# Two levels of Strassen instead of one in the first channel product, with outer sums added on the way out of PSUM

## The chip, the cores and the metric

The kernel runs on one core of a Trainium2 chip. Five engines work beside each other, each through its own list of instructions in order: TensorE (PE; its weight loads are shown apart as PEld), VectorE (DVE), ScalarE (ACT), GpSimd (POOL) and SyncE (SP), whose list issues nearly all DMAs. SBUF holds tiles of 128 partitions; matmuls write PSUM, which has eight banks of 512 float32 columns. The metric is the device time of one execution in microseconds. Three runs of the kernel before took 1167.77, 1168.61 and 1169.41 us; the median is 1168.61.

## The reference

Two blocks follow each other, all in float32.

```python
# attention: q, k, v are (8, 8, 576, 64), omega is (128, 64)
q_p, k_p = (phi(q_s), phi(k_s))       # exp(h - max h) / sqrt(m), h = x @ omega.T - |x|^2 / 2
kv = np.einsum('bhsm,bhsd->bhmd', k_p, v)
num = np.einsum('bhsm,bhmd->bhsd', q_p, kv)
den = np.einsum('bhsm,bhm->bhs', q_p, z)[..., None] + 1e-06
# bridge: (8, 8, 576, 64) -> x of (8, 576, 512); then a Fourier mix and a channel MLP
X = np.fft.fft(np.fft.fft(x, axis=1), axis=2)
u = x + np.real(X)
un = (u - mu) / np.sqrt(var + 1e-06)
ch = np.maximum(un @ w_ch1, 0.0) @ w_ch2      # w_ch1 (512, 2048), w_ch2 (2048, 512)
return u + ch
```

The change concerns the first of the two products of the last lines, `un @ w_ch1` with its relu: 4608 tokens, 512 channels in, 2048 hidden channels out.

## The kernel before

The kernel has two stages. In the first (to 424 us of the profile) it does the attention, the Fourier mix and four plain tiles of 128 tokens of the MLP. It also prepares for the second stage: the weights w1 stay in SBUF, and the sums that the second channel product needs of w2 are written to DRAM as 49 tiles of 256 KB (`w2l`).

In the second stage the other 4096 tokens go through the MLP in eight blocks (j = 0 to 7) of 512 tokens. A product of matrices is computed by Strassen's scheme in Winograd's form: the two operands are cut into 2 x 2 parts, sums of the parts are formed (`sums_left`, `sums_right`), seven products of half size are taken instead of eight, and the four parts of the result are sums of these. The products are numbered 1 to 7 in the code; 1, 2, 4 and 7 have a left factor that is a part or a simple difference, 5, 6 and 3 have sums.

The first channel product of a block uses one level. The left factor is w1 (channels by hidden, transposed by the matmul), the right one the normalized tokens `unT`. `first_of(j, fc)` does one of eight slices of 2 x 128 hidden channels: seven products of two matmuls each, 128 hidden channels by 256 tokens. Three results are saved from PSUM by ACT (`save`, L1324), three are evicted by DVE, which adds the saved one and applies the relu in one custom operation (`added`, L1296), and one goes out by ACT (L1362). They land in `hid`. POOL then forms the four sums of hidden parts that the second product needs (L1377). The weight sums (`weight_sums`, L1254) are made once and stay in SBUF as `w1s`.

The second channel product of a block uses two levels, 7 x 7 products ("leaves") of four matmuls, 128 tokens by 128 channels each. `product_of(j, i)` does the seven leaves of one outer product i; DVE forms the inner sums of hidden tokens (`add_up`, L1457), ACT and DVE empty PSUM (L1465, L1470, L1523), and POOL or DVE add the outer product's result into the residual rows (`plus`, L1530). The 49 weight tiles are read from DRAM again for each block (`loads_w2`, L1393) into twelve buffers (`wl`), so that SP's list reads ahead by up to twelve leaves.

While a block is computed, the next one is normalized: rows are read back from DRAM, DVE takes mean and variance (L1022 to L1024), POOL the power -1/2 (L1026), DVE scales (L1028) and transposes 32 x 32 blocks (L972), and the rows go through DRAM once more to arrive as `unT` (L980, L988).

The order of instructions on each engine is planned when the kernel is built. Work is written as streams of `Step`s, each with an engine, an estimated time, events that it waits for and buffers that it takes and gives. `Listing.run` takes the step that can begin first by these estimates, with small biases. In the first stage a string of picks (`PICKS`) fixes the choice. The estimates include a resource `PORT`: a step marked `port=True` on DVE or POOL is planned to start only when the last such step of either engine has ended. Three outer products or slices may be under way together (`set`).

## Time and profile before

| what | value |
|---|---|
| median of three runs | 1168.61 us |
| the profiled execution: span, the only time that the page gives of it | 1172.2 us |
| PE busy | 1153.5 us (98%) |
| DVE, ACT, POOL busy | 754.7, 436.8, 430.4 us |
| DMA | 220.34 MB, mean 188 GB/s |
| first stage, 0 to 424 us: PE, DVE, POOL busy | 413.4, 339.7, 173.9 us |
| block 3 (701.0 to 794.6 us): PE, DVE, ACT, POOL busy | 92.6, 52.6, 19.4, 32.5 us |

A line of the page names the program's line, the engine, the operation and the tiles (written <- read). Busy times of different engines overlap each other. In the chain of waits each piece ended last at its time, so that its lines add up to the span. "Idle before" is time that an engine spent waiting just before an instruction of a group, with the engine or DMA that ended the wait.

### The profile page before, as it was taken

To read this page: it belongs to the slowest core of one execution; us is meant where nothing else is said; L and a number is where in the kernel's file an instruction comes from. 1 tells how busy PE (TensorE), PEld (TensorE's weight loads), DVE (VectorE), ACT (ScalarE), POOL (GpSimd) and SP (SyncE) were. 2 spreads that over 40 slices of the span, in tenths; PEclk is the share of its full clock that TensorE was granted. 3 is DMA by queue.
4 is the path that set the end of the run, shared out by engine and by line. 5 is a ranking of instruction groups with operands and counts; after the bars stand their busy time and mean duration, and the time that the engine had idled before them with its cause. 6 is when DMAs were issued, how large, how long until landed. Compare 5 with 4: busy or idle time off the path is not lost.

```text
span 1172.2 us, 31328 instructions
## 1 busy us (share of the span) xinstructions
PE 1153.5 (98%) x12437; PEld 1032.9 (88%) x12437; DVE 754.7 (64%) x1573; ACT 436.8 (37%) x1485; POOL 430.4 (37%) x496
## 2 busy tenths in 40 slices
PE   8999999999999999999999999999999999999998
PEld 7888888779777868998998998898999899899898
DVE  5999999986676655744754664573573574474255
ACT  6998898866444212122112212212212212221211
POOL 2433444455472106225225324413513512522421
PEclk8999999999999999999999999999999999999999
DMA  7866765665662254873783593694495396388055
GB/s 218 224 188 186 240 181 178 203 210 163 207 196 101 77 162 139 263 264 85 222 278 112 172 308 99 152 317 141 112 319 190 82 290 231 83 258 263 35 166 203
DMA packets 167217, 220.34 MB, mean 188 GB/s; under 512 B 50080, under 2 KB 81056, under 8 KB 167072
## 3 DMA queue, kind: packets, MB, share of 16 engines
q1 hardware_dynamic: 166576, 218.09, 60.7%
q8 instruction: 98, 1.61, 0.6%
q14 instruction: 47, 0.39, 0.1%
q10 hardware_dynamic: 496, 0.26, 0.1%
HBM read 179.24 MB, written 43.25 MB: 190 GB/s over the span
## 4 chain that ended last, share of the span: by engine, by line
PE 88%; DMA 5%; DVE 4%; ACT 2%; SPq 1%; issue 1%; DVEq 0%
PE banks L1310 33%; PE banks L1490 27%; PE banks L1099 5%; PE banks L606 5%; PE banks L1122 4%; PE banks L512 4%; DMA wl<-w2l 3%; PE banks L640 2%; PE banks L687 2%; PE banks L849 2%; PE banks L799 1%; ACT e L566 1%; DVE nmx L549 1%; DMA kq<-in_k_dram 1%; PE banks L809 1%; PE banks L860 1%
## 5 line engine op out<-in xcount | busy, mean ns | idle before, releaser
L1490 PE MATMUL banks<-wl,sums 128*128 128x128 f32 x1792 | 217.4, 275 | 0.0
L1490 PEld LDWEIGHTS banks<-wl,sums 128*128 128x128 f32 x1792 | 208.6, 192 | 0.0
L1296 DVE CUSTOM_DVE_ANT_0 hid<-banks,s 128x256 f32<-128x256 f32 x192 | 80.9, 424 | 188.8 <-PE banks L1310 188.8
L566 ACT ACTIVATE e<-banks,nmx 128x128 f32<-128x128 f32 x576 | 165.3, 434 | 23.2 <-DVE nmx L549 22.4
L1324 ACT ACTIVATE s<-banks 128x256 f32<-128x256 f32 x192 | 73.7, 384 | 259.0 <-PE banks L1310 259.0
L1310 PE MATMUL banks<-unT,w 128*128 128x256 f32 x704 | 166.3, 379 | 0.0
L1310 PEld LDWEIGHTS banks<-unT,w 128*128 128x128 f32 x704 | 133.2, 190 | 18.3 <-issue 0.5
L1530 POOL TENSOR_TENSOR ur<-ur,part 128x512 f32<-128x512 f32 x32 | 47.3, 1479 | 267.1 <-ACT part L1523 187.0
L1465 ACT ACTIVATE s<-banks 128x128 f32<-128x128 f32 x168 | 46.6, 278 | 256.7 <-PE banks L1490 220.3
L1310 PE MATMUL banks<-tt,w1s 128*128 128x256 f32 x512 | 126.3, 379 | 0.0
L1310 PEld LDWEIGHTS banks<-tt,w1s 128*128 128x128 f32 x512 | 97.0, 190 | 13.7 <-DVE hid L1296 0.4
L1490 PE MATMUL banks<-wl,hid 128*128 128x128 f32 x768 | 100.0, 276 | 3.2 <-DMA wl<-w2l 3.1
L1470 DVE TENSOR_TENSOR part<-banks,s 128x128 f32<-128x128 f32 x168 | 49.0, 292 | 83.4 <-PE banks L1490 82.2
L549 DVE TENSOR_REDUCE nmx<-banks 128x8 f32<-128x1024 f32 (+1 forms) x96 | 89.3, 951 | 19.7 <-PE banks L606 15.5
L1490 PEld LDWEIGHTS banks<-wl,hid 128*128 128x128 f32 x768 | 94.0, 192 | 6.0 <-DMA wl<-w2l 4.5
L606 PE MATMUL banks<-om,kqT 64*64 64x128 f32 (+1 forms) x2088 | 80.6, 278 | 1.9 <-ACT kv L656 1.2
L1310 PE MATMUL banks<-unT,w1s 128*128 128x256 f32 x320 | 79.5, 379 | 0.0
L606 PEld LDWEIGHTS banks<-om,kqT 64*64 64x64 f32 (+1 forms) x2088 | 65.8, 140 | 13.3 <-issue 4.3
L1490 PE MATMUL banks<-wl,hs 128*128 128x128 f32 x576 | 75.1, 275 | 0.5 <-DVE part L1470 0.4
L1490 PEld LDWEIGHTS banks<-wl,hs 128*128 128x128 f32 x576 | 70.1, 192 | 1.2 <-DVE part L1470 0.6
L1377 POOL TENSOR_TENSOR hs<-hid,hs 128x256 f32<-128x256 f32 x64 | 50.1, 784 | 57.2 <-issue 37.1
L1310 PEld LDWEIGHTS banks<-unT,w1s 128*128 128x128 f32 x320 | 60.4, 190 | 8.7
(128 smaller groups left out, 1914.6 us busy)
## 6 DMA issues: line engine op xcount, KB each, us to landing
wl<-w2l SPq DMA_DIRECT2D x392, 256.0 KB
raw<-in_moe_w_ch_dram SPq DMA_DIRECT2D x32, 512.0 KB
kq<-in_k_dram SPq DMA_DIRECT2D x32, 288.0 KB
kq<-in_q_dram SPq DMA_DIRECT2D x32, 288.0 KB
vd<-in_v_dram SPq DMA_DIRECT2D x32, 288.0 KB
u<-us SPq DMA_DIRECT2D x36, 256.0 KB
ur<-us SPq DMA_DIRECT2D x36, 256.0 KB
out_dram<-ur SPq DMA_DIRECT2D x34, 256.0 KB
```

The source lines that it names most:

```text
L512: nc.tensor.transpose(ps[:, (j - j0) * 128 : (j - j0 + 1) * 128], src(j), ident[:])
L549: nc.vector.tensor_reduce(nmx[:, :, 0:num], pps[:, :, 0 : MF * num].rearrange("p b (c m) -> p b c m", m=MF), axis=AX.X, op=ALU.max, negate ...
L566: nc.scalar.activation(out=e[:, c + (i if num == 1 else 0), :], in_=pps[:, i, MF * c : MF * c + MF], func=AF.Exp, bias=nmx[:, i, c : c + 1],)
L606: nc.tensor.matmul(pps[cols, c, MF * m : MF * m + MF], lhsT=kqT[rows, j, cols], rhs=om2[rows, :],)
L1099: nc.tensor.matmul(hp[:, 0:TP], lhsT=w1[:, dc, 128 * fc : 128 * fc + 128], rhs=unTs[key][:, dc, :], start=(dc == 0), stop=(dc == NDC - 1),)
L1296: nc.vector._custom_dve(TENSOR_ADD_SAT, out=o, in0=ps, in1=sb, s0=FMAX, s1=0.0)
L1310: nc.tensor.matmul(ps[:, 0:HT].rearrange("f (b q) -> f b q", q=Q), lhsT=left(dc), rhs=right(dc), start=start and dc == 0, stop=(dc == D2 - 1),
L1324: nc.scalar.activation(out=s[:], in_=ps[:, 0:HT], func=AF.Copy)
L1377: nc.gpsimd.tensor_tensor(out=o, in0=l, in1=r, op=op)
L1470: nc.vector.tensor_tensor(out=part[:, t, 128 * m : 128 * m + 128], in0=ps[:, 0:128], in1=saved[with_][:], op=ALU.add,)
L1490: nc.tensor.matmul(ps[:, 0:128], lhsT=left[:, f], rhs=wls[j, i, n][:, f], start=start and f == 0, stop=(f == 3), skip_group_check=True,)
L1530: eng.tensor_tensor(out=o, in0=o, in1=other, op=ALU.add)
```

## The change

The first channel product now uses two levels in six of its seven outer products (in block 0: in one of the seven; the others, product 5 in every block and products 2 to 7 in block 0, stay undivided at the second level and are listed by `single`). `first_of(j, i)` does one outer product i over all 1024 hidden channels and 256 tokens of its part. A divided one has seven leaves of four matmuls, each 128 hidden channels by 128 tokens over 128 channels; the undivided one has sixteen matmuls of 256 tokens.

Outer products are no longer kept apart until all are there. Where one adds to an earlier result (`merged`: 6, 2, 7, 3, 4), DVE adds that result while it empties PSUM, and the last of each part (`final`: 2, 3, 4) gets the relu there too. Two sums are left for POOL (`u4_row`, `last_row`, the latter with a relu on ACT). `hid` is now four cells in the layout of the outer parts, and the four sums for the second product are formed in place in it by POOL (`left_sums`), each after the second product that still reads the cell.

DVE forms the inner sums of tokens for each block (`token_sums`). The weight sums of the outer products stay in SBUF (`so`, and one difference in place in w1); those of the inner level are formed in block 0 (`w1_sums`), stored to DRAM as 15 tiles of 256 KB (`w1l`), and read for each of blocks 1 to 7 into the same twelve buffers as the w2 tiles (`load_leaves`).

Besides: the second products are taken in another order, ACT instead of DVE scales the rows of the next block, saves of the second product have five buffers of their own (`sq`), the planner no longer regards `PORT` in the second stage, and streams have ranks that decide between steps that could start at the same time.

```diff
-SECOND = Clock(190.0, 0.15, 0.0, 0.1, {}, {}, (PE, ACT, DVE, POOL, SP, NONE), {})
+SECOND = Clock(190.0, 0.15, 0.0, 0.1, {}, {}, (PE, ACT, DVE, POOL, SP, NONE), {}, False)
...
-            return max(t, u, self.free[e] if e != NONE else 0.0, self.free[PORT] if step.on_port(e) else 0.0)
+            return max(t, u, self.free[e] if e != NONE else 0.0, self.free[PORT] if clock.port and step.on_port(e) else 0.0)
...
         nc.vector.bn_aggr(out=mv[:], in_=st[:])
         nc.vector.tensor_scalar(rstd[:], mv[:, 1:2], 1e-6, None, op0=ALU.add)
...
+        if block:
+            nc.vector.tensor_scalar(mv[:, 0:1], mv[:, 0:1], -1.0, None, op0=ALU.mult)
...
+        if block:
+            nc.gpsimd.tensor_tensor(mv[:, 0:1], mv[:, 0:1], rstd[:], op=ALU.mult)
+            yield Step(ACT, 0.6)
+            nc.scalar.activation(out=u[:], in_=u[:], func=AF.Identity, bias=mv[:, 0:1], scale=rstd[:])
+            yield from by_blocks(j, i, pool, u, *block)
+            return
         yield Step(DVE, 0.455, port=True)
         nc.vector.tensor_scalar(u[:], u[:], mv[:, 0:1], rstd[:], op0=ALU.subtract, op1=ALU.mult)
-        if block:
-            yield from by_blocks(j, i, pool, u, *block)
...
+    NB, TBIAS = 0.0, 0.6
+    ORDER1 = (1, 6, 5, 2, 7, 3, 4)
+    ORDER0 = (1, 2, 6, 5, 7, 3, 4)
+    def single(j):
+        return (5,) if j else ORDER0[1:]
+    def twice(j):
+        return tuple(i for i in ORDER1[1:] if i not in single(j))
...
+    def inner_tokens(j, i):
+        b11, b21, b22, b12 = (tokens(j, i, n) for n in (1, 2, 3, 7))
+        for o, l, r, op in sums_right(b11, b12, b21, b22, *(tokens(j, i, n) for n in (5, 6, 4))):
+            yield lambda o=o, l=l, r=r, op=op: nc.vector.tensor_tensor(out=o, in0=l, in1=r, op=op)
+    def token_sums(j):
+        if j == 1:
+            yield Step(NONE, after=tuple(("w1l", i, n) for i in twice(1) for n in (5, 6, 3)))
+        for i in (ORDER1 if j else ORDER0)[1:]:
+            if i in single(j):
+                continue
+            for m, op in enumerate(inner_tokens(j, i)):
+                yield Step(DVE, 0.28, after=(("tt", j),), makes=("tokens", j, i) if m == 3 else None, port=True, bias=TBIAS if j else -2.0)
+                op()
...
         for i, (o, l, r, op) in enumerate(ops):
-            yield Step(DVE, 0.6, makes=("tt", j) if i == 3 else None, port=True, bias=-0.49)
+            last = i == 3
+            yield Step(DVE, 2.0 if last else 0.7, makes=("tt", j) if last else None, port=True, bias=-0.49)
             nc.vector.tensor_tensor(out=o, in0=l, in1=r, op=op)
+            if last:
+                for inner in inner_tokens(j, 1):
+                    inner()
+        if pool is not mlpp:
+            yield from token_sums(j)
...
     listing.buffers = {k: [0.0] * n for k, n in dict(
-        slab=0, u=2, turn=1, ht=NFC, ur=3, s=6, set=3, wl=NWL, sums=NSUM, part=4,
+        slab=0, u=2, turn=1, ur=3, s=6, sq=5, set=3, wl=NWL, sums=NSUM, part=4,
     ).items()}
-    w1s += [late.tile([128, 3, D2, GW], F32, name=f"w1s{g}") for g in range(1, 4)]
-    hid = late.tile([128, NFC, TB], F32, name="hid")
-    hs = late.tile([128, HF, 3, HT], F32, name="hs")
+    hid = late.tile([128, 4, 2, 2, 4 * P], F32, name="hid")
+    so.update({i: late.tile([128, D2, F2], F32, name=f"so{i}") for i in (5, 6, 3)})
+    rx = late.tile([128, 6, 3, 4, Q], F32, name="rx")
...
+    READ = {1: 5, 6: 3, 5: 6, "u4": 7}
+    WITH = {6: C11, 2: C11, 7: C21, 3: C12, 4: C21}
+    BEFORE = {6: 1, 2: 1, 7: 6, 3: "u4", 4: 7}
...
+    def first_of(j, i):
+        me = ("first", j, i)
+        slot, read = slot_of(j, i), READ.get(i)
+        free = ((("second", j - 1, read), "read"),) if read and j else ()
+        merged, final = i in WITH, i in (2, 3, 4)
+        addend = slot_of(j, 1) if i in (6, 2) else WITH.get(i)
+        kept = {}
...
+            left, right = weights_of(j, i, n), tokens(j, i, n)
+            for f in range(4):
                 nc.tensor.matmul(
...
+                    ps[:, P * f : P * f + P].rearrange("f (b q) -> f b q", q=Q),
+                    lhsT=left[:, P * f : P * f + P],
+                    rhs=right,
+                    start=start and f == 0,
+                    stop=True,
                     skip_group_check=True,
                 )
...
+        def save(name, ps, f, t):
+            if merged:
+                yield Step(DVE, 0.7, 0.1, take=("s",), after=with_(f, t), makes=(me, name))
+            else:
+                yield Step(ACT, 0.6, 0.1, take=("s",), makes=(me, name))
+            s = late.tile([128, 4 * P], F32, name="s", tag="s", bufs=6)
+            if merged:
+                nc.vector.tensor_tensor(out=s[:], in0=ps, in1=cell_of(addend, f, t), op=ALU.add)
+            else:
+                nc.scalar.activation(out=s[:], in_=ps, func=AF.Copy)
+            kept[name] = s
+        def added(name, f, t, ps, saved, give, after=()):
+            yield Step(
+                DVE, 0.7, 0.1, after=((me, saved),) + free + over(f, t) + after, makes=(me, name), give=give + ("s",)
+            )
+            o = cell_of(slot, f, t)
+            if final:
+                relu_sum(o, ps, kept[saved][:])
+            else:
+                nc.vector.tensor_tensor(out=o, in0=ps, in1=kept[saved][:], op=ALU.add)
+            yield Fork(rest(f, t, (me, name)))
...
+        def u4_row(f, here):
+            read = ((("second", j - 1, READ["u4"]), "read"),) if j else tuple(
+                ("h", j, n, f, t) for n in (2, 6) for t in range(2)
+            )
+            yield from add(
+                row_of(C12, f), row_of(C21, f), row_of(slot, f), ALU.add,
+                after=here + read + tuple(("h", j, 6, f, t) for t in range(2)),
+            )
...
+                        cell = ps.rearrange("p (t n) -> p t n", t=2)[:, :, 128 * n : 128 * n + 128]
+                        for d in range(2):
+                            col = GW * f + 256 * c + 128 * n
+                            nc.tensor.matmul(
+                                cell.rearrange("f t (b q) -> f t b q", q=Q),
+                                lhsT=w[:, d, col : col + 128],
+                                rhs=right[:, :, d].rearrange("f (t b) q -> f t b q", t=2),
+                                start=n == 0 and d == 0,
+                                stop=d == 1,
+                                skip_group_check=True,
...
+        xb, x = yield from leaf(1, None, True, take=bank)
+        yield Fork(save("p1", x, 0, 0))
...
+    def left_sums(j):
+        for n, o, l, r, op, after in (
+            (3, C12, C11, C12, ALU.subtract, lambda f, t: (("h", j, 2, f, t), ("h", j, 3, f, t))),
+            (2, C22, C22, C12, ALU.subtract, lambda f, t: ((("second", j, 4), "read"), ("S", j, 3, f, t))),
+            (1, C11, C22, C11, ALU.add, lambda f, t: ((("second", j, 1), "read"), ("S", j, 2, f, t))),
+            (4, C21, C21, C22, ALU.subtract, lambda f, t: ((("second", j, 2), "read"), ("S", j, 2, f, t))),
+        ):
+            for f in range(2):
+                yield from add(*(row_of(c, f) for c in (o, l, r)), op, after=after(f, 0) + after(f, 1))
+                for t in range(2):
+                    yield Step(NONE, makes=("S", j, n, f, t))
...
+            nc.sync.dma_start(w1l[i][(5, 6, 3).index(n)], w)
...
+        yield Step(NONE, after=(("us", B - 1), "converted"))
+        for s in sums:
+            yield from outer(*s, parts)
+        yield Step(NONE, after=tuple(("op", n) for n in range(NPLAIN)))
+        yield from outer(7, a[1], a[7], ALU.subtract, parts)
+        for m, i in enumerate(i for i in ORDER0 if i in twice(1)):
+            yield Step(NONE, after=((("first", 0, i), "leaves"),))
+            yield from inner(m, i)
+            for n in (1, 2, 4):
...
+    def order(j):
+        return (4, 1, 2, 6, 5, 3, 7) if j < NTB - 1 else (4, 1, 2, 6, 7, 5, 3)
...
+    def load_leaves():
         for j in range(NTB):
-            for i in ORDER:
+            for i in twice(j):
+                for n in (5, 6, 3):
+                    yield Step(SP, 0.45, 2.6, take=("wl",), after=(("w1l", i, n),), kb=165, makes=("wx", j, i, n))
+                    wx = late.tile([128, GW], F32, name="wx", tag="wl", bufs=NWL)
+                    nc.sync.dma_start(wx[:], w1l[i][(5, 6, 3).index(n)])
+                    wxs[j, i, n] = wx
+            for i in order(j):
                 for n, l in enumerate(PARTS):
...
-        return lambda t, f: hid[:, g + 4 * f : g + 4 * f + 4, t0 + 128 * t : t0 + 128 * t + 128]
+        c = {1: C11, 2: C21, 4: C22, 7: C12, 6: C22, 5: C11, 3: C21}[i]
...
     def halves():
         for j in range(NTB):
-            for fc in range(HF):
-                yield Step(NONE, take=("set", "ht", "ht"))
-                yield Fork(first_of(j, fc))
+            for n, i in enumerate(ORDER1 if j else ORDER0):
+                yield Step(NONE, take=("set",))
+                yield Fork(first_of(j, i), 2 + rank(j, 0, n))
+            yield Fork(read_up(j))
+            yield Fork(left_sums(j))
             cells = {}
             yield Fork(second_of(j, cells))
-            for i in ORDER:
+            for n, i in enumerate(order(j)):
                 yield Step(NONE, take=("set",))
-                yield Fork(product_of(j, i, cells))
+                yield Fork(product_of(j, i, cells), 2 + rank(j, 1, n))
...
+    listing.run([late_turns(), late_norms(), halves(), load_leaves(), token_sums(0), w1_sums()])
```

## The prediction

> **What bounds the kernel now.** I read the busy shares first, then the chain of waits, then the windows around one block of the second stage (from 424 us on, eight blocks of 512 tokens), then the groups and the timeline there.

> ```profile
> span 1172.2 us, 31328 instructions
> ...
> PE 1153.5 (98%) x12437; PEld 1032.9 (88%) x12437; DVE 754.7 (64%) x1573; ACT 436.8 (37%) x1485; POOL 430.4 (37%) x496
> ...
> PE banks L1310 33%; PE banks L1490 27%; PE banks L1099 5%; PE banks L606 5%; PE banks L1122 4%; PE banks L512 4%; DMA wl<-w2l 3%; PE banks L640 2%; PE banks L687 2%; PE banks L849 2%; PE banks L799 1%; ACT e L566 1%; DVE nmx L549 1%; DMA kq<-in_k_dram 1%; PE banks L809 1%; PE banks L860 1%
> ```
> TensorE is the bound, and two lines are 60% of the chain: L1310, the first channel product, and L1490, the second.

> ```profile
> 659.84 41.31 PE banks L1490 x368
> ...
> 707.23 36.26 PE banks L1310 x168
> ...
> 753.66 5.73 DMA wl<-w2l
> ```
> These pieces of the chain, unbroken, give the pitch: L1490 (128 columns) 41.31/368 = 112.3 ns, L1310 (256 columns) 36.26/168 = 215.8 ns. A matmul of the program is two instructions.

> ```profile
> 659.84:701.15 41.31, 41.31 (x369) 41.16 (x369) 29.49 (x56) 7.33 (x26) 8.43 (x7) 1.00 0.96 306
> 701.15:753.66 52.51, 52.51 (x264) 46.65 (x263) 24.36 (x51) 12.47 (x35) 25.52 (x36) 1.00 0.38 113
> ```
> One second product, one first: window, PE, PEld, DVE, ACT, POOL busy, clock, DMA share, GB/s. The clock is full; the second product nearly fills the DMA engines (0.96), the first leaves them at 0.38.

> ```profile
> PE banks L1490 <- DMA wl<-w2l: 3.1, 5, 1.4
> PE banks L1490 <- DVE part L1470: 0.4, 1, 0.4
> ...
> SPq L980 <- DVE turn L972: 155.6, 27, 10.9
> ```
> From 424 us on TensorE waits 3.5 us in all. Last, SP's queue stands behind DVE's transposes for 156 us without harm: twelve weight tiles are ahead.

> ```profile
> 751.03 0.69 DVE L1457 TENSOR_TENSOR sums<-hid 128x512 f32<-128x512 f32 x1
> 751.75 1.10 DVE L1457 TENSOR_TENSOR sums<-sums,hid 128x512 f32<-128x512 f32 x1
> ...
> 755.06 0.68 DVE L1457 TENSOR_TENSOR sums<-sums,hid 128x512 f32<-128x512 f32 x1
> 755.66 0.68 DVE L1457 TENSOR_TENSOR sums<-hid 128x512 f32<-128x512 f32 x1
> ```
> DVE alone takes 0.68 us with 0.60 from start to start; beside a POOL sum (751.13 to 753.44 us) the same work took 1.10, and POOL's 256 columns 1.17 instead of 0.73. Evictions, one input in PSUM, do not show this: L1296's mean is 0.424 us with or without POOL beside it.

> **TensorE.** Before, a block's first product is 7 x 8 x 2 = 112 matmuls, 224 instructions x 215.8 = 48.3 us. After, in blocks 1 to 7, six outer products of 7 x 4 matmuls of 128 columns are 336 instructions x 112.3 = 37.7 us, and the undivided one is 16 matmuls of 256 columns, 32 x 215.8 = 6.9: together 44.6, 3.7 less. Block 0 divides only product 1: 56 x 112.3 + 192 x 215.8 = 47.7, 0.6 less. In all 7 x 3.7 + 0.6 = 26.5 us, on the path. The 128-column pitch is from L1490, same shape and operand kinds; L1099, also 128 columns but in the first stage, ran 40 in 4.66 us = 116.5. That end costs 2408 x 4.2 ns = 10.1 us; I take 112.3, the neighbour in the same stage.

> **Evictions.** DVE: 24 x 0.424 = 10.2 us a block become 38 of 512 columns. Not shown for the custom operation; L1135 (PSUM and SBUF, 512) took 0.689 and the slope from 292 ns (L1470) to 424 ns gives 0.69, so 26.2. ACT loses 32 x 0.38 = 12.2 us and gets 8 copies at 0.64 (L528) and two relus of 1024 columns, some 7.5. POOL: 32 x 0.78 = 25 become 12 sums of 1024 columns at 2.36 (L743), 28; DVE's sums beside them stretch these, below. The planner no longer keeps DVE and POOL apart in this stage.

> **Token sums and norms.** 24 DVE sums of 128 columns at 0.284 (L1422): +6.8 us. The scaling L1028, 4 x 0.94 = 3.8, goes to ACT at some 0.64 each, for 4 x 0.15 more on DVE (as L1024) and as many small POOL products (0.55, L1026). L1457 reads whole rows now, 0.685 each. DVE per block: 26.2 + 6.8 + 28 x 0.685 + 21 x 0.292 + 6 x 0.687 (L1530) + 7.5 (norms) + 2.7 (L1171) = 72.6 us, against 52.6 before, in 88.6 of TensorE. Cover is left, unevenly: by the changed kernel's order the tight stretch runs from product 2 to the end of product 4. TensorE does 28 first and 10 second leaves, 38 x 0.898 = 34.1 us; DVE 28 evictions (19.3), three norms with transposes (5.6), 8 sums (5.5), 5 small ones (1.9): 32.3 at full durations, some 28 at the pitch above. Following it leaf by leaf, each eviction (TensorE to DVE 0.20 us, at 434.14 and 434.34) ends before the leaf that needs it, often by under 1 us. Bounds 0 and 3.7 us per block; I take 0.3.

> **POOL's chain.** `left_sums` starts when product 3's last eviction is in, and its eight sums wait on the second products 4, 1, 2. Product 5, fifth in order, needs five of them 16.8 us later: 5 x 2.36 = 11.8 alone, plus 0.45 for each DVE sum that collides (1.10 - 0.68, or 1.17 - 0.73), about ten: 16.3. It just fits; 0.2 us per block.

> **Loads.** 15 tiles of 256 KB more per block, and SP passes 15 more issues (0.3 to 0.4 us each). The leaf order keeps twelve tiles ahead; a second product still draws 49. The first product's window rises from 113 GB/s x 52.5 us = 5.9 MB to 9.9 MB, 205 GB/s, below the 306 shown. Bounds: nothing, or 3.9 MB / 306 = 12.8 us per block; the 0.38 share is nearest, so nothing.

> **Block 0.** The 12 sums of L1254 become 36 (22 DVE, 14 POOL) and 15 stores; weight loads queue on SP behind these stores, which wait for POOL. DVE has 25 us of evictions and sums in 47.7, but the norm that precedes product 6's sums waited 3.4 us for its load before (L1022). Bounds 0 and 6; I take 1.5. The first stage stands in the same order on every engine, but for four sums of 0.28 on an idle DVE; the end has the same steps.

> **Sum.** 1172.2 - 26.5 + 7 x 0.5 + 1.5 = 1150.7. The page gives no time beside its span, and that is 0.3% above the median of the runs, 1168.61; by the ratio 0.9969, **1147 us**. Its range: all hidden, and today's 3.5 us of waits gone, 1139; the slower pitch, 1157; with 0.3 us per block more, 1159.

> **The rivals.**
> - *POOL becomes the bound of the second product.* If every sum is stretched as the worst row, 1.17/0.73, a sum is 3.8 us and five 19: 2.2 late in seven blocks, 15.4 more, 1162. For: 18.8 us of POOL now lie where DVE sums most. Against: only the colliding part is stretched. 0.12.
> - *DVE becomes the bound, and it is slower.* In-order DVE could pay the 0.20 hand-off before each of the tight stretch's 28 evictions: 32.3 + 5.6 = 37.9 against 34.1, 3.8 per block, 26.6 us: 1172. It decides from 3.7 us per block. For: 95% full at full durations. Against: the 0.60 pitch. [...] 0.09.
> - *The loads do not hide:* 7 x 12.8 = 90 us, 1234. For: 0.96 in the second product. Against: 0.38 in the first. 0.06.
> - *Weight loads set the pitch.* Halving columns doubles loads per column; if a leaf ran at PEld's mean of 190 ns, 336 x 78 ns = 26 us per block, 1325. PEld is busy 41.16 of 41.31 us, yet the pitch stays 112.3: 0.04. [...]
> - *That the change does less than it says:* the built order holds the counts above, so no chance. Something else, slower: 0.03.

> **How the numbers follow.** Forecast 0.66. A measurement of this kernel tells 0.2%, 2.3 us, from no change. Faster: 0.66 + 0.12 + 0.02 of the DVE rival (it lies on the line) = 0.80; same 0.03 of it; slower 0.04 + 0.06 + 0.04 + 0.03 = 0.17. The range 1139 to 1170 leaves out 0.17 above and some 0.03 below.

> **What would show it.** Right: from block 1 on a period near 89 us; leaves at 112 ns; TensorE's waits under 1 us per block. Wrong: waits of leaves on DVE evictions in products 2, 7, 3, 4 (DVE rival); of product 5's leaves or `sums2` on POOL (POOL rival); on `wx` or `wl` (loads); a pitch above 120 ns (weight loads).

## The result, and the profile after

The changed kernel takes 1260.5 us (1259.13 to 1263.23) against 1169.01 us of the kernel before on the same chip: 1.0782 times as long, with a 95% interval of 1.0757 to 1.0807. The forecast of 1147 us, and its range up to 1170, were wrong by far, and the change goes the other way.

First the page of the changed kernel: span, busy shares, then the chain by engine and by line.

```profile
span 1258.0 us, 33698 instructions
...
PE 1160.3 (92%) x13469; PEld 1067.8 (85%) x13469; DVE 997.0 (79%) x1845; ACT 421.1 (33%) x1337; POOL 511.9 (41%) x385
...
PE 64%; DVE 20%; DMA 7%; issue 5%; ACT 3%; SPq 1%; DVEq 0%; POOL 0%; ACTq 0%; POOLq 0%
PE banks L1754 23%; PE banks L1419 10%; PE banks L1542 5%; DVE sums L1721 5%; PE banks L1105 5%; DMA u<-us 5%; PE banks L607 4%; PE banks L1128 4%; PE banks L513 4%; PE banks L641 2%; PE banks L688 2%; DVE s L1442 2%; DVE hid L1365 2%; PE banks L850 2%; DVE tt L1192 1%
```

The chain of the kernel before, by engine:

```profile
PE 88%; DMA 5%; DVE 4%; ACT 2%; SPq 1%; issue 1%; DVEq 0%
```

TensorE's busy share of the span fell from 98% to 92%, and DVE, 4% of the chain before, is 20% of it. Two windows of one block say where: the unbroken part of the second product (288 of its 392 matmul instructions), then that of the first product. Columns: window, length, then busy time of PE, PEld, DVE, ACT, POOL, the granted clock, the DMA share, GB/s.

```profile
900.40:945.59 45.19, 36.65 (x290) 35.78 (x289) 35.31 (x50) 5.56 (x20) 22.08 (x11) 0.92 0.80 227
847.79:887.83 40.04, 40.04 (x330) 39.21 (x329) 32.90 (x69) 9.84 (x14) 13.61 (x13) 1.00 0.62 189
```

The first product is as forecast: TensorE is busy in all of its 40.04 us. In the second, 288 leaves' instructions at 112.3 ns would take 32.3 us and take 45.2. POOL is busy for 22.08 us there; in the second product before it was 8.43 of 41.31. The groups of DVE's sums and of two of its evictions, and of POOL's long sums (busy time, mean ns of one):

```profile
L1386 POOL TENSOR_TENSOR hid<-hid 128x1024 f32<-128x1024 f32 x96 | 240.7, 2519 | 241.2 <-DVE hid L1365 62.5 <-ACT hid L1520 60.1 <-PE banks L1754 43.7
L1721 DVE TENSOR_TENSOR sums<-hid 128x512 f32<-128x512 f32 x112 | 106.5, 955 | 0.2 <-ACT hid L1495 0.2
L1721 DVE TENSOR_TENSOR sums<-hid,sums 128x512 f32<-128x512 f32 x56 | 83.1, 1483 | 16.2 <-PE banks L1754 16.1
L1442 DVE TENSOR_TENSOR s<-banks,hid 128x512 f32<-128x512 f32 x105 | 69.3, 683 | 13.9 <-PE banks L1419 13.4
L1721 DVE TENSOR_TENSOR sums<-sums,hid 128x512 f32<-128x512 f32 x56 | 60.8, 1085 | 0.9
```

Evictions of 512 columns, one input in PSUM, take 0.683 us against 0.69 forecast. The sums of line 1721, the same number of columns but both inputs in SBUF, were forecast at 0.685 and take 0.96 to 1.48 in the mean. The timeline shows why. First a POOL sum and the DVE sum that meets it; then another, with a DVE sum of only 128 columns.

```profile
886.58 2.35 POOL L1386 TENSOR_TENSOR hid<-hid 128x1024 f32<-128x1024 f32 x1 [1.22 <-DVE hid L1365]
...
887.02 2.46 DVE L1721 TENSOR_TENSOR sums<-hid 128x512 f32<-128x512 f32 x1
```

```profile
921.45 2.46 POOL L1386 TENSOR_TENSOR hid<-hid 128x1024 f32<-128x1024 f32 x1 [5.44 <-PE banks L1754]
921.74 2.32 DVE L1192 TENSOR_TENSOR tt<-unT,tt 128x128 f32<-128x128 f32 x1
```

POOL's first sum ends at 888.93 and DVE's at 889.48, 0.55 us later. The small one takes 2.32 us instead of 0.28 and ends 0.15 us after POOL's. So these DVE sums are not slowed by some share: read this way, each stands still until the POOL instruction ends, then runs. Counted over the second stage of the trace: 148 of the 224 sums of line 1721 begin while no POOL sum runs and average 0.682 us, none above 0.70; 76 begin beside one, average 1.97 us, and every one ends 0.55 us (0.545 to 0.554) after that POOL sum. 43 of them met a sum of 1024 columns and took 2.45 us each. Above 0.683 us each, the held sums lose 97.9 us in all; in the trace before, 23 of 224 are held and lose 12.8.

The way from there to TensorE, in the same block:

```profile
906.03 0.28 DVE L1734 TENSOR_TENSOR part<-banks,s 128x128 f32<-128x128 f32 x1
906.23 2.63 DVE L1721 TENSOR_TENSOR sums<-sums,hid 128x512 f32<-128x512 f32 x1
...
908.78 0.28 DVE L1734 TENSOR_TENSOR part<-banks,s 128x128 f32<-128x128 f32 x1
...
909.12 1.23 PE L1754 MATMUL banks<-wl,hid 128*128 128x128 f32 x6 [2.75 <-DVE part L1734]
```

The eviction at 908.78 stood behind the held sum on DVE, the next leaf stood behind the eviction, and TensorE was idle for 2.75 us. What follows such a stall is in two windows, first the 3.3 us after this one, then a window a little later:

```profile
909.60:912.90 3.30, 3.30 (x18) 3.30 (x17) 0.38 (x3) 0.28 (x1) 1.99 (x1) 0.50 0.68 205
...
913.20:915.20 2.00, 2.00 (x20) 2.00 (x19) 2.00 (x2) 0.56 (x2) 2.00 (x2) 1.00 0.69 162
```

The granted clock is 0.50, and the matmuls stand 0.213 us apart instead of 0.111. It comes back after some 3.4 us. In most blocks this happens twice. By the starts of the second stage's matmuls, counted against their pitch, TensorE loses some 93 us in gaps and 31 us to the slower pitch; by the trace's clock records 61 us of that stage run at 0.50, which comes to the same 31.

The longest waits of TensorE from 424 us on (total, times, longest):

```profile
PE banks L1754 <- issue: 30.7, 11, 7.9
PE banks L1754 <- DVE part L1734: 21.2, 9, 3.5
PE banks L1754 <- DVE sums L1721: 12.9, 6, 2.2
PE banks L1754 <- ACT s L1729: 12.4, 16, 1.3
PE banks L1419 <- DVE hid L1365: 3.7, 6, 0.7
```

Nearly all lie in the second product (L1754), and none of them names a load. "Issue" is no cause of its own here: all eleven of its waits end 0.10 us after a DVE instruction, ten of them a sum of line 1721, and eight of those a held one, as the leaf at 903.45 us after the sum of 900.52.

Block lengths, worked out from the starts of the blocks' first leaves (us; the forecast column is the length before, less 3.7 and plus 0.5, or less 0.6 and plus 1.5 in block 0):

| blocks | before | forecast | after |
|---|---|---|---|
| 0 and 1 together | 184.9 | 182.6 | 217.6 |
| 2 to 6, mean | 93.1 | 89.9 | 102.3 |
| 7 | 93.8 | 90.6 | 104.7 |

### The profile page after: what moved, and what is told of

The parts are those of the page before. It is cut to its first block, busy times and chain, and to the rows that moved or that the text cites. A ratio compares the mean times of both kernels' runs of the same rounds, so it can differ in the third digit from the quotient of the medians.

```text
span 1258.0 us, 33698 instructions
## 1 busy us (share of the span) xinstructions
PE 1160.3 (92%) x13469; PEld 1067.8 (85%) x13469; DVE 997.0 (79%) x1845; ACT 421.1 (33%) x1337; POOL 511.9 (41%) x385
## 3 DMA queue, kind: packets, MB, share of 16 engines
q8 instruction: 107, 1.75, 0.6%
## 4 chain that ended last, share of the span: by engine, by line
PE 64%; DVE 20%; DMA 7%; issue 5%; ACT 3%; SPq 1%; DVEq 0%; POOL 0%; ACTq 0%; POOLq 0%
PE banks L1754 23%; PE banks L1419 10%; PE banks L1542 5%; DVE sums L1721 5%; PE banks L1105 5%; DMA u<-us 5%; PE banks L607 4%; PE banks L1128 4%; PE banks L513 4%; PE banks L641 2%; PE banks L688 2%; DVE s L1442 2%; DVE hid L1365 2%; PE banks L850 2%; DVE tt L1192 1%
## 5 line engine op out<-in xcount | busy, mean ns | idle before, releaser
L1386 POOL TENSOR_TENSOR hid<-hid 128x1024 f32<-128x1024 f32 x96 | 240.7, 2519 | 241.2 <-DVE hid L1365 62.5
L1754 PE MATMUL banks<-wl,sums 128*128 128x128 f32 x1792 | 239.9, 290 | 54.3 <-issue 29.0
L1754 PEld LDWEIGHTS banks<-wl,sums 128*128 128x128 f32 x1792 | 227.0, 205 | 59.7 <-issue 31.1
L1754 PE MATMUL banks<-wl,hid 128*128 128x128 f32 x1344 | 177.5, 286 | 22.8 <-DVE part L1734 21.2
L1754 PEld LDWEIGHTS banks<-wl,hid 128*128 128x128 f32 x1344 | 167.5, 201 | 24.9 <-DVE part L1734 22.9
L1721 DVE TENSOR_TENSOR sums<-hid 128x512 f32<-128x512 f32 x112 | 106.5, 955 | 0.2 <-ACT hid L1495 0.2
L1721 DVE TENSOR_TENSOR sums<-hid,sums 128x512 f32<-128x512 f32 x56 | 83.1, 1483 | 16.2 <-PE banks L1754 16.1
L1442 DVE TENSOR_TENSOR s<-banks,hid 128x512 f32<-128x512 f32 x105 | 69.3, 683 | 13.9 <-PE banks L1419 13.4
L1419 PE MATMUL banks<-rx,wx 128*128 128x128 f32 x560 | 71.7, 275 | 0.0
L1419 PEld LDWEIGHTS banks<-rx,wx 128*128 128x128 f32 x560 | 67.0, 192 | 0.0
L1542 PE MATMUL banks<-tt,so 128*128 128x256 f32 x288 | 66.5, 380 | 0.2 <-DVE so L1386 0.2
L1105 PEld LDWEIGHTS banks<-unT,w 128*128 128x128 f32 x512 | 60.2, 192 | 4.4 <-issue 2.3
```

The lines of the kernel that those rows point to most:

```text
L1105: nc.tensor.matmul(hp[:, 0:TP], lhsT=w1[:, dc, 128 * fc : 128 * fc + 128], rhs=unTs[key][:, dc, :], start=(dc == 0), stop=(dc == NDC - 1),)
L1386: eng.tensor_tensor(out=o, in0=l, in1=r, op=op)
L1419: nc.tensor.matmul(ps[:, P * f : P * f + P].rearrange("f (b q) -> f b q", q=Q), lhsT=left[:, P * f : P * f + P], rhs=right, start=start an ...
L1442: nc.vector.tensor_tensor(out=s[:], in0=ps, in1=cell_of(addend, f, t), op=ALU.add)
L1542: nc.tensor.matmul(cell.rearrange("f t (b q) -> f t b q", q=Q), lhsT=w[:, d, col : col + 128], rhs=right[:, :, d].rearrange("f (t b) q -> ...
L1721: nc.vector.tensor_tensor(out=o, in0=l, in1=r, op=op)
```

## The experiments

The theory to test is the hold: POOL's sums stop DVE's sums for the rest of their own length. The first rival: the leaves wait for the results of POOL's sums, which come late. Others: DVE is full whatever POOL does (46 evictions of 512 columns a block by the prediction's count, 38 by DVE and 8 by ACT, are 23,552 columns); the 15 additional loads; the planner's lost rule.

### The left sums left out, unread, in pieces; the loads left out

```
# "..." stands for code not shown; add() gets an argument `to` in e1 and e2
# e1: the eight sums are not issued        e2: they write where nobody reads
  yield from add(..., op, to=False, ...)   yield from add(..., op, to=ur1[:].bitcast(mybir.dt.bfloat16), ...)
# e3: each POOL sum of 1024 columns as four of 256
+ w = o.shape[-1] // 4 if o.shape[-1] == 1024 else o.shape[-1]
+ for c in range(0, o.shape[-1], w):
+     eng.tensor_tensor(out=o[:, c : c + w], in0=l[:, c : c + w], in1=r[:, c : c + w], op=op)
# e4: no loads of weight sums
- wx = late.tile([128, GW], F32, name="wx", tag="wl", bufs=NWL)
- nc.sync.dma_start(wx[:], w1l[i][(5, 6, 3).index(n)])
- wxs[j, i, n] = wx
+ wxs[j, i, n] = w1s[:, (5, 6, 3).index(n)]
```

> The changed kernel with the eight POOL sums of left_sums left out of every block (64 of the 96 POOL sums of 1024 columns; the second products 7, 6, 5 and 3 then read the unsummed rows); every other instruction stands in the same order on its engine. Hold theory: a DVE sum with both inputs in SBUF that starts while POOL runs a sum waits until that POOL instruction ends (duration = what POOL has left + 0.55 us in the trace after), DVE is in order, and the leaves behind its evictions wait too: 13.9 us per block. Without these POOL sums only the holds by ur's 512-column sums remain, 1 to 2 us per block: 1160 us (1150 to 1172). Late-POOL theory (the leaves wait for the results of the POOL sums themselves): the same 1160. DVE theory (DVE is too full with 23,552 PSUM columns, whatever POOL does): 1240 or more. Loads theory (the 15 more tiles per block): 1255 to 1262.

> The changed kernel, the eight POOL sums of left_sums still run from the same inputs, in the same order, but write to a tile that nobody reads (in bf16, so that it fits), so that no leaf and no DVE sum waits for a POOL sum's result; what they read is the unsummed rows. Hold theory: POOL's sums hold DVE as before, so the time stays: 1260 (1235 to 1265), and DVE's sums of the second product keep a mean over 0.95 us. Late-POOL theory: the waits go, 1160 (1150 to 1175). Loads theory: 1260.

> The changed kernel, every POOL sum of 1024 columns issued as four of 256, nothing else moved. Hold theory: a colliding DVE sum now waits for the rest of a 0.73 us instruction instead of one of 2.4 us; the holds fall to a half or less, though DVE and POOL then alternate and POOL's chain grows: 1205 us (1170 to 1230), no DVE sum above 1.35 us. Late-POOL theory: POOL's chain is 4 x 0.73 = 2.9 us a sum instead of 2.4 to 2.65, five sums 1.5 to 2.5 us later in each block: 1272 to 1285. Loads and DVE theories: 1255 to 1265.

> The changed kernel without the 15 loads of weight sums per block (blocks 1 to 7; the first product's inner leaves then read a resident tile instead, wrong weights). Hold theory: the loads are hidden, 1260 (1252 to 1265). Loads theory (DMA at 0.77 to 0.80 in the second product is what slows it): below 1200.

Measured, with the ratio to the kernel before (1170.29 us in these runs):

| run | us | ratio and interval |
|---|---|---|
| e1, sums left out | 1164.21 | 0.9944 (0.9926 to 0.9962) |
| e2, sums unread | 1250.95 | 1.0687 (1.0659 to 1.0716) |
| e3, four pieces | 1211.66 | 1.0352 (1.0326 to 1.0378) |
| e4, no loads | 1256.82 | 1.0734 (1.0700 to 1.0767) |

e1 and e2 together decide between the hold and the late results. Without POOL's eight sums 96 of the changed kernel's 1260.5 us go; with the sums running but nobody waiting for them, 9.6 go. So some 87 of the 96 us are the sums' mere presence, and waiting for their results is about a tenth. (It can be a little more: e2's sums write bf16 and take 2.60 us instead of 2.52, so its holds are somewhat longer.) All other parts of the change stand in e1 as they are, and it is no slower than the kernel before. The groups of e2 show DVE held as in the changed kernel, though nothing reads the results of POOL's sums; and neither in e2 nor in the changed kernel does a wait of TensorE or DVE in the second stage name POOL:

```profile
L1387 POOL TENSOR_TENSOR ur<-hid 128x1024 bf16<-128x1024 f32 x64 | 166.7, 2604 | 66.8 <-DVE hid L1365 63.3
L1722 DVE TENSOR_TENSOR sums<-hid 128x512 f32<-128x512 f32 x112 | 122.6, 1099 | 0.2 <-ACT hid L1496 0.2
L1722 DVE TENSOR_TENSOR sums<-hid,sums 128x512 f32<-128x512 f32 x56 | 83.7, 1494 | 14.0 <-PE banks L1755 14.0
```

And in e1 the second product's window, with DVE and POOL far less busy and the clock full:

```profile
761.71:795.68 33.97, 32.63 (x290) 32.31 (x289) 24.82 (x49) 5.54 (x20) 6.61 (x5) 1.00 0.98 306
```

That is 34.0 us for the piece that took 45.2, with DMA at 306 GB/s, so DMA has the room. DVE, with all of its evictions and sums, is busy for 24.8 us of it: it is not too full. e3 went in the direction that only the hold expects: POOL works longer (0.905 us a piece in the mean, 3.6 for what took 2.52), and the kernel gets 49 us faster. The bound of 1.35 us for a DVE sum was a miss: some reach 1.76, beside `ur`'s sums of 512 columns, which were not cut. e4's interval overlaps that of the changed kernel: the loads were hidden, or cost a few us at most.

### A copy in the sums' place

```
# e5, on e2: for the eight sums, a POOL copy with one input (...)
- eng.tensor_tensor(out=to, in0=l, in1=r, op=op)
+ eng.tensor_copy(out=to, in_=l)
```

> As the kernel whose left sums nobody waits for (1250.95 us), but each of these 64 POOL sums is a POOL copy of 1024 columns with one SBUF input, at the same place in POOL's order (the sums themselves are left out). If the hold is between instructions that both read two SBUF inputs (port theory): DVE's sums run at 0.6 to 0.7 us beside the copies and the time is that of the kernel without the sums, 1164 us (1158 to 1172). If any POOL instruction holds DVE's sums: the holds shrink only with the length of the copy, 1200 to 1250.

1174.45 us, 1.0044 (1.0027 to 1.0060), between the two expectations and outside both. The groups and the trace settle it:

```profile
L1390 POOL CAST ur<-hid 128x1024 bf16<-128x1024 f32 x64 | 78.9, 1233 | 51.8 <-DVE hid L1365 49.3
```

38 sums of DVE that met such a copy are held, and each ends 0.54 to 0.55 us after it. So here a POOL copy with one SBUF input holds as a sum with two does; the theory that two inputs are needed on both sides fell. The cost is small because the copy is half as long (1.23 us against 2.60) and so meets fewer sums and holds each for less. How the time grows with the hold: 1164 us without, 1174 with instructions of 1.2 us, 1251 with 2.6. Above 0.683 us each, the held sums lose 20.6, 47.5 and 113.4 us in these three: the first 27 us more cost the kernel 10, the next 66 cost 77. That DVE's slack hides the first ones is my reading, and no run tests it alone.

### Other places for the sums, and the planner's rule

```
# e6: left_sums on DVE
  yield from add(*(row_of(c, f) for c in (o, l, r)), op, (DVE,), ...)
# e7: POOL or DVE by the planner, POOL's in pieces of 256
  yield from add(*(row_of(c, f) for c in (o, l, r)), op, (POOL, DVE), ...)
# e8: the planner's rule back
- SECOND = Clock(190.0, 0.15, 0.0, 0.1, {}, {}, (PE, ACT, DVE, POOL, SP, NONE), {}, False)
+ SECOND = Clock(190.0, 0.15, 0.0, 0.1, {}, {}, (PE, ACT, DVE, POOL, SP, NONE), {}, True)
```

> The changed kernel with the eight sums of left_sums on DVE instead of POOL, the order of all engines planned anew. Hold theory: the long holds go; DVE gets 8 x 1.25 = 10 us more per block, and in the second product it was busy 37.2 of 45 us without these sums, so it becomes the bound there, by 2 to 6 us per block: 1196 us (1175 to 1215). DVE theory (DVE was too full already): 1270 or more.

> The changed kernel with the planner free to put the sums of left_sums on POOL or DVE (it puts two to three of eight on DVE) and every POOL sum of 1024 columns as four of 256. Hold theory: fewer and shorter holds than with the four pieces alone (1211.66 us), for some 3 us more of DVE work: 1197 us (1180 to 1212).

> One part of the change undone: the planner again keeps DVE's and POOL's two-input sums apart in the second stage; the rest is as changed. If the planner's lost rule is what cost the time, this comes near the forecast: below 1180 us. Hold theory: the two engines' sums are one resource, and the second product asks it for 8 x 2.4 + 5 x 1.3 on POOL and some 27 us on DVE, 53 us in 45 us of leaves; keeping them apart only writes the waits into the order: no gain, 1260 us or more.

e6: 1214.68 us, 1.0385 (1.0349 to 1.0422), at the upper end of its range; e7: 1213.72, 1.0367 (1.0337 to 1.0397), no better than four pieces alone and just above its range. e8: 1362.97 in its one run, far slower: with the rule back, the orders write out the waits (TensorE waits 22.7 us for POOL's sums and 29.8 us for loads of weight tiles). Putting the rule back does not win the time back; that there is no room for what it asks rests on the sum in the expectation. What limits e6 stays open: from 600 us on, TensorE's longest waits there name loads of weight tiles (12.0 us) and DVE's sums (10.1). None of these beats the kernel before, and e1 says why: even with the sums for nothing the gain would be 0.6%.

### The hold in the kernel before

The last two runs leave the change out and try the suspected cause alone.

```
# e9: in the second stage DVE's and POOL's sums may overlap in the plan
- if step.on_port(eng):
+ if clock is FIRST and step.on_port(eng):
# ... and the same condition where begin() reads self.free[PORT]
# e10, on e9: sums of four feature blocks in one POOL instruction (with the steps' times and events, not shown)
+ if fc % 4 != 3:
+     return
+ four, four2 = slice(fc - 3, fc + 1), slice(HF + fc - 3, HF + fc + 1)
- lo[:, t1], hi[:, t1], lo[:, t2], hi[:, t2], *(hs[:, fc, i] for i in range(3))
+ hid[:, four, t1], hid[:, four2, t1], hid[:, four, t2], hid[:, four2, t2],
+ *(hs[:, four, i] for i in range(3)),
```

> The kernel before with one part of the change alone: the planner no longer keeps DVE's and POOL's two-input sums apart in the second stage. POOL's sums stay 256 columns long (0.73 us) and lie in the first product, where DVE mostly reads PSUM. Hold theory: a held DVE sum waits 0.73 us at most and DVE has 20 us of slack per block: 1171 us (1167 to 1177). If the planner's rule by itself was worth much: above 1185.

> As the kernel before without the rule that keeps the sums apart, but the POOL sums hs of four feature blocks in one instruction: 8 sums of 1024 columns (2.36 us) per block instead of 32 of 256, 19 us of POOL instead of 23; the last four run beside the second product's first DVE sums. Hold theory: DVE's sums<-hid there are held up to 2.4 us each, two to four of them per block, and leaves wait behind them: 2 to 5 us per block, 1195 us (1180 to 1215). Late-POOL theory: the last sum is ready 10 us after the first product, the first leaf that needs it comes 19 us after it: 1170 us (1166 to 1175).

e9: 1178.67 us, 1.0086 (1.0057 to 1.0116), just above its range; the rule was worth more than expected, some 10 us. e10: 1246.69 us, 1.0676 (1.0648 to 1.0705). Only the grouping of POOL's sums separates it from e9, and POOL even works less (384.9 us against 419.0), yet the kernel is 68 us slower. The hold theory had the sign and was far too low: it put e10 24 us above e9, and 68 were measured. Above 0.683 us each, the held sums lose 69.5 us in e10 against 20.2 in e9, more than the 2 to 5 us a block expected, and what follows a stall was not priced. TensorE's waits from 424 us on, and two groups of POOL and DVE:

```profile
PE banks L1496 <- DVE part L1476: 44.7, 17, 4.8
PE banks L1496 <- ACT s L1471: 5.0, 8, 0.6
```

```profile
L1463 DVE TENSOR_TENSOR sums<-hid 128x512 f32<-128x512 f32 x64 | 86.1, 1355 | 0.3
...
L1382 POOL TENSOR_TENSOR hs<-hid,hs 128x1024 f32<-128x1024 f32 x16 | 41.2, 2576 | 0.0
```

Four DVE sums a block are held by these, 32 in all, each ending 0.55 us after its POOL sum, and evictions and leaves queue behind them exactly as in the changed kernel. The mean clock falls from 0.998 in e9 to 0.969.

## Why the prediction was wrong

- **What bounds the kernel now, and TensorE's part: right.** The first product is 44.5 us a block (the 40.04 us window and five leaves that lie apart); 44.6 were forecast, by a pitch of 112.3 ns. The rival of the weight loads never came up: sixteen matmul instructions of L1419 took 1.786 us from 886.05 us on, 112 ns each.
- **Evictions: right.** 0.675 to 0.689 us against 0.69, and POOL beside them changes nothing (L1442: 0.681 with a POOL sum beside it, 0.685 without). The first product, in which the forecast saw DVE's tight stretch, runs without a wait to speak of.
- **"L1457 reads whole rows now, 0.685 each": wrong.** This put DVE's 72.6 us a block together from times of sums that meet nothing, though the change moves 19 us of POOL's work from beside evictions to beside those very sums. Held, they cost 97.9 us more over the kernel.
- **"Plus 0.45 for each DVE sum that collides": the step that failed.** 0.45 came from 1.10 - 0.68 and 1.17 - 0.73, collisions with POOL sums of 256 columns, and was carried over to sums of 1024 as a toll per collision. For POOL this was near: 42 of its 96 sums begin while DVE runs a sum from SBUF, and these take 2.73 us instead of 2.36. For DVE it is no toll but the rest of POOL's instruction, 1.77 us for each sum that met 1024 columns, and the prediction charged DVE, where the leaves wait, nothing for it. Of the 113 us between forecast and result, e1 puts 96 on these POOL sums; of the 17 that are left, 12.6 lie in blocks 0 and 1. The trace of before had the evidence. What the prediction reads as one POOL sum from 751.13 to 753.44 us is two; the first ends at 752.30 us, and the DVE sum of 751.75, which takes 1.10, at 752.85, 0.55 us after it. These two lines of it show a POOL sum of 512 columns ending at 589.51 and the DVE sum at 590.06, 0.55 us later:

```profile
587.82 1.69 POOL L1530 TENSOR_TENSOR ur<-ur,part 128x512 f32<-128x512 f32 x1 [18.33 <-ACT part L1523]
...
588.30 1.76 DVE L1457 TENSOR_TENSOR sums<-hs 128x512 f32<-128x512 f32 x1
```

  All 23 held sums of that trace end so. Had I set ends beside ends, and not compared durations, the price would have read, as an estimate: up to 2.36 us, the length of L743's sum, for each sum that meets a 1024-column sum.
- **POOL's chain "just fits", 0.2 us a block: nearly right.** Waiting for POOL's results is worth some 10 us in all (e2). The POOL rival (1162 us) asked for the wrong thing.
- **The DVE rival (1172 us): right engine, wrong mechanism.** It priced DVE as too full in the first product, by hand-offs. DVE was held in the second, where a plain sum of durations left cover: 24.8 of 34.0 us (e1).
- **Loads at nothing: right** (e4).
- **Block 0, 1.5 us: wrong, in part by the same step.** In the changed kernel blocks 0 and 1 take 35.0 us more than forecast. Even in e1 they take 195.2, 12.6 more than forecast, and there TensorE stands 7.9 us in one place, at 503 us: three of DVE's token sums in a row take 1.63 to 1.75 us beside POOL's weight sums of 512 columns. That is some 3.1 us of hold; the rest is DVE's order, in which eight token sums stand ahead of the sum that the leaf needs. Without left sums, blocks 2 to 6 average 89.5 us against the forecast's 89.9: the rest of the sum stood.
- **What follows a stall: missed.** The clock, halved for 3.4 us or twice that after many of the stalls, costs 31 us in all and was in no term.

## What to carry to other kernels

In the traces of both kernels DVE's 512-column sums with both inputs in SBUF that were held beside a POOL sum (76 of 224 after, 23 of 224 before) ended 0.55 us after it, and those of the changed kernel took 1.97 us on average instead of 0.682; so price each meeting by the length of the POOL instruction, and look for it by comparing end times, not means. Before giving POOL longer instructions or moving them, ask what DVE runs beside them at the new place: here evictions from PSUM were not slowed (0.681 us beside a POOL sum, 0.685 without), sums from SBUF were held, and what stood behind a held sum on DVE waited too (TensorE for 2.75 us behind the eviction of 908.78 us). If such work has to be there, short instructions on POOL lost less here (1211.66 us in pieces of 256 columns against 1260.5), though none of the layouts tried won back the gain.

## What was not expected of the hardware

```profile
923.27:926.68 3.41, 1.27 (x11) 1.08 (x11) 3.41 (x6) 0.20 (x1) 1.91 (x2) 1.00 0.83 257
926.68:930.10 3.42, 3.42 (x18) 3.42 (x18) 1.66 (x6) 0.00 (x0) 0.00 (x0) 0.50 0.24 85
```

```profile
786.72:790.13 3.41, 1.48 (x14) 1.28 (x12) 2.64 (x6) 0.00 (x0) 0.00 (x0) 1.00 1.10 245
790.13:793.54 3.41, 2.34 (x21) 2.37 (x22) 2.81 (x5) 0.55 (x2) 0.77 (x1) 1.00 1.04 333
```

  Counted over the second stages of these two traces: 16 stretches at full clock have 2.12 us or more without a matmul, and each is followed by one at 0.50; none with under 1.70 us is; of the three in between (1.72, 1.79 and 1.91 us), the one of 1.72 is.
